# The first third of a hand-written order laid out anew, in a fused retention and wave-MLP kernel

## The chip, the cores and the metric

The kernel runs on one core of a Trainium2 chip. The metric is the device time of one execution in microseconds. The core's engines are TensorE (PE: matrix products and transposes), VectorE (DVE), ScalarE (ACT) and GpSimd (POOL); SyncE (SP) issues most of the transfers, ScalarE and GpSimd issue the others. All transfers share 16 DMA engines.

## The reference

Two stages. The first is a linear attention with a decay for each head, over q, k and v of shape 4 × 8 × 768 × 64. The second, on its output laid out as x of 4 × 768 × 512, is a mixing of phases over tokens and a mixing over channels.

```python
for t in range(S):
    state = gamma[None, :, None, None] * state + np.einsum('bhd,bhe->bhde', k[:, :, t], v[:, :, t])
    y[:, :, t] = scale * np.einsum('bhd,bhde->bhe', q[:, :, t], state)
...
theta = x @ w_theta
zr, zi = x * np.cos(theta), x * np.sin(theta)
y = np.einsum('ts,bsd->btd', w_tok_r, zr) + np.einsum('ts,bsd->btd', w_tok_i, zi)
u = x + y
return u + np.maximum(u @ w_ch, 0.0)
```

## The kernel before

The order of the work is not left to a scheduler. `ORDER` is a string of 929 tokens, and the last loop of the kernel calls the function that each token names, in that order. A token such as `ck.2.a` is a function (`ck`), a number (unit 2) and, where there is a choice, an engine: `a` ScalarE, `v` VectorE, `p` GpSimd, `s` SyncE. Each engine executes its own instructions in the order in which the tokens issue them; between engines, semaphores hold the data dependences. So the place of a token decides what stands behind it on its own engine, and nothing else.

**Attention.** The work is cut into 24 units: batch b, a third i of the tokens (256 of them) and half of the heads h, with n = 2 (3 b + i) + h. For each unit:

- `Lk`, `Lq`, `Lv` load 256 KB each of k, q and v. The loads of SyncE and ScalarE take turns on eight semaphores.
- `ck` casts k to bf16; `cq` casts q (in units 0 to 3, 7, 9 and 10, among others, `cqs` multiplies it with the decay instead); `cv` multiplies v with its decay. All three write what PE reads (`kqb`, `vb`).
- `Tk`, `Tq` transpose on PE into one PSUM tile, `E` copies it to SBUF (`kqT`).
- `A` makes the 16 small products of q and k (`at_ps`, one PSUM buffer), `m` masks them on VectorE (`at`, 1024 columns).
- `ST` adds up k-v states in columns of the PSUM banks R0 and R1 of the unit; `S0`, `S1` carry the state on to the next third of the tokens, and `SB.n.g` copies it to bf16 for `I`, the product of q with the old state. `Y` adds the product with `at` in the same banks.
- `XB` (after `cqs`) copies the result out of R0 or R1 to `xT`; `XA` (after `cq`) multiplies it with the decay on the way. The result of unit n stands in the banks beside the states of unit n + 1, so `I` of unit n + 1 can write to them only after `XB` or `XA` of unit n.

**Mixing.** For each tile C of 128 tokens: `Tx` transposes `xT` and `Ex` copies it (or `Dx` does both by DMA), `Hh` makes theta on PE with the weights `wth`, `CN` takes sine and cosine on ScalarE, `z` multiplies both with x. `Tw.r.t` transposes a row tile of a token weight matrix (r = 0 real, 1 imaginary), `Ew` copies it. `M.t.s` adds two products into row tile t; `u`, `Tu`, `Eu` (or `Du`), `O` and `f` are the channel mixing with the weights `wch`, and `SO` stores.

**Weights.** `Pth` loads w_theta, `Pch` w_ch, and `Pw.r.g` the token weights in groups of row tiles: g = 0 is row tile 0, g = 1 is row tiles 1 and 2, g = 2 is row tiles 3 to 5. GpSimd issues all of them, in order with its own operations, and they are cast from f32 to bf16 on the way.

**Others.** `const…` prepare constants; `const9` and `const8` are four activations each that fill the table `qx` (const8 256 columns, those of the first third of the tokens, const9 the 512 of the others), which `XA` alone reads; `const7` brings the table of the sine into ScalarE. `Z` is two products of zeros on PE, to nothing.

In the order before, the changed part has 338 tokens and ends at `M.4.5`; it holds the attention of units 0 to 8 in full and parts of units 9 and 10, and row tiles 0 to 2 of batch 0 with a part of tile 3.

Of the kernel before, what the change touches and what calls it, by code (L numbers as in the profile page):

```python
# [34 lines left out]
CN.3.0 Tx.4 CN.3.1 Ew.0.0.v S0.6.v XA.5.1 Ex.4.v Hh.4 CN.4.0 CN.4.1 Tw.0.1 M.0.1 Pw.1.1 z.3.v M.0.0
Tw.0.2 Pw.1.2 Ew.0.2.a SB.6.1.a Hh.5 z.4.p SB.6.0.p Lk.9.a M.0.3 ck.7.p cqs.7.p M.0.2 CN.5.1 CN.5.0
cq.8.v m.6 Ew.0.1.v Tw.1.1 Tw.1.2 Ew.1.1.v Lv.9.s M.0.4 M.1.0 Tx.5 Ew.1.2.v M.1.1 S1.6 Tk.7 M.1.4
Pch Ex.5.v z.5.v cv.7.v Tq.8 Tq.7 M.1.2 E.7.a M.0.5 I.6 Y.6 ST.7 A.7 ck.8.a u.0 S0.7.v m.7 XA.6.1
SB.7.1.a M.1.5 M.1.3 XA.6.0 Tw.1.3 M.2.5 Pw.0.2 M.2.3 u.1 S1.7 Tk.8 M.2.1 M.2.0 SB.7.0.v Ew.1.3.a
Tu.0 I.7 cv.8.v E.8.a Lk.10.s ck.10.p cv.9.p Y.7 ST.8 A.8 cqs.9.v ck.9.v M.2.4 Du.1 Eu.0.a XB.7.1.a  # L40
XB.7.0.v S0.8.v SB.8.0.v M.2.2 Tx.6 Tq.9 Tk.9 Lv.10.a cv.10.p Lq.10.s S1.8 u.2 m.8 O.0 E.9.a
SB.8.1.a Hh.6 Tw.1.4 I.8 Y.8 A.9 CN.6.0 Du.2 Lq.14.s CN.6.1 Ex.6.v f.0 ST.9 Tw.0.3 Hh.7 Ew.1.4.v
Ew.0.3.a S0.9.v Tw.0.4 M.3.0 Tw.1.5 CN.7.0 CN.7.1 M.3.2 Dx.7 M.3.1 M.3.5 M.3.3 Lv.12.s Lk.12.s
Ew.1.5.v XA.8.1 Ew.0.4.v Lq.12.s M.3.4 u.3 S1.9 Tw.0.5 Tk.10 M.4.5 cqs.10.p XA.8.0 m.9 M.4.3 Tq.10
SB.9.1.a SB.9.0.a I.9 O.2 Lq.11.s Lk.11.s E.10.a Lk.15.s Ew.0.5.v Lk.14.s Y.9 ST.10 A.10 z.7.p
Lv.11.s XB.9.1.a XB.9.0.a f.2 M.4.0 O.1 M.4.1 cqs.14.p m.10 S0.10.v f.1 cq.11.a ck.12.v M.4.4 M.4.2
Tu.3 Eu.3.a Dx.9 SB.10.0.a cqs.12.p u.4 Hh.9 Tq.11 ck.11.v Tu.4 z.6.v Eu.4.v ck.15.v M.5.0 M.5.4
Tk.11 E.11.a SB.10.1.p cv.11.p M.5.2 M.5.3 I.10 M.5.5 M.5.1 Lq.13.a A.11 Y.10 ck.14.v ST.11 CN.9.1
CN.9.0 SO.0.a Hh.8 u.5 S0.11.v z.9.v XB.10.0.v m.11 Dk.12 Tx.8 Tq.14 O.4 Lv.13.a SB.11.0.a Lq.15.s
Lk.13.s CN.8.1 Lk.18.a XB.10.1.a CN.8.0 SB.11.1.p cv.12.p Lq.16.s I.11 Tk.14 Ex.8.v A.12 Y.11 ST.12  # L50
f.4 Lv.15.s O.3 z.8.p E.14.a XA.11.0 XA.11.1 Hh.10 S0.12.a f.3 SB.12.0.v Tx.10 Tu.5 CN.10.1 Dx.11
Ex.10.v cq.13.p Lk.16.s Lv.17.s Hh.11 SO.2.s CN.10.0 m.12 S1.12 z.10.v Tk.15 M.6.1 M.6.2 M.6.0 M.6.3
CN.11.0 CN.11.1 M.7.3 SB.12.1.a Lk.17.a ck.13.a M.7.4 M.7.0 M.6.4 Dk.13 M.7.1 z.11.v M.6.5 SO.3.s
A.14 M.7.2 Eu.5.v I.12 Lv.14.s u.6 cqs.15.v M.7.5 M.9.3 Tq.15 ck.17.a E.15.a m.14 SO.4.a Lq.17.s
Lq.18.s Lk.21.s ck.16.a M.9.0 M.9.5 M.9.1 M.9.4 Lq.19.a M.9.2 Du.6 cv.13.v u.7 M.8.0 u.9 Y.12
cv.14.p ST.13 A.13 O.5 XB.12.1.a XB.12.0.a M.8.1 S0.13.a S1.13 M.8.4 M.8.3 SB.13.0.a SB.13.1.p
cq.16.p m.13 I.13 ck.18.a Y.13 ST.14 A.15 f.5 cq.17.v Lv.18.a M.8.5 M.8.2 XA.13.0 XA.13.1 S0.14.v
SB.14.0.p Lv.16.s Hh.13 S1.14 u.8 Tx.12 M.10.1 cv.15.p cv.17.p SB.14.1.p M.10.0 M.10.4 cqs.18.v
M.10.5 CN.13.0 CN.13.1 Hh.12 CN.12.1 I.14 m.15 Y.14 CN.12.0 ST.15 S0.15.v XB.14.1.a SB.15.0.a M.10.3
cv.16.v Dk.16 Dk.17 Du.7 Dx.13 M.10.2 Dk.18 O.6 SB.15.1.p XB.14.0.v S1.15 I.15 Y.15 ST.16 SO.5.a  # L60
cv.18.p f.6 S0.16.v A.16 M.11.4 SB.16.1.p M.11.1 Lq.21.a Ex.12.a z.12.p SB.16.0.a Lk.19.s Lk.20.s
XB.15.0.a u.10 z.13.p XB.15.1.a m.16 O.7 Du.10 I.16 Y.16 ST.17 f.7 A.17 Tu.8 Hh.15 CN.15.1 CN.15.0
Dx.14 M.11.2 Tx.15 Lv.22.s SO.7.s M.11.0 M.11.5 S0.17.v SB.17.0.p M.11.3 XA.16.1 m.17 XA.16.0
Ex.15.v Hh.14 SB.17.1.p z.15.p cq.19.p ck.21.p Eu.8.a ck.19.p I.17 u.11 Tu.11 A.18 Y.17 ST.18
# [7 lines left out]
cv.21.v u.14 A.21 ST.21 CN.19.0 CN.19.1 S0.21.v M.15.3 M.15.5 S1.21 m.21 XA.20.1 Hh.18 CN.18.1  # L72
CN.18.0 Dx.18 Dk.22 ck.23.a M.15.4 M.15.2 SB.21.0.p M.15.1 M.15.0 SB.21.1.v Lv.23.s Du.12 Dx.19
XA.20.0 O.9 f.9 I.21 Y.21 A.22 ST.22 M.16.1 cqs.23.p u.15 m.22 S0.22.v z.18.p z.19.p M.16.5
SB.22.0.p M.16.4 O.12 M.16.0 SO.8.a M.16.2 M.16.3 SB.22.1.p XB.21.0.a XB.21.1.a SO.11.s Du.14
cv.23.p Dk.23 f.12 Du.13 Dx.20 Dx.21 Hh.21 u.16 I.22 A.23 Y.22 ST.23 CN.21.0 CN.21.1 Hh.20 CN.20.1
# [6 lines left out]
Mh.1.0 Mh.1.4 u.22 O.18 Mh.1.3 SO.15.a f.19 M.20.0 M.20.1 Tuh.0 u.21 Du.22 Du.21 f.18 M.20.3 Euh.0
M.20.4 Mh.1.1 M.20.5 u.20 O.22 Mh.1.5 uh.1 f.22 Tu.20 SO.14.a SO.19.s Eu.20.a O.21 SO.18.a Tuh.1
Euh.1 f.21 Oa.0 Oa.1 fa.0 fa.1 Oh.0 Oh.1 SO.21.a SO.22.s SO.20.s fh.0 SOh.0 fh.1 SOh.1 Z.31
""".split()


# [558 lines left out]
```

## Time and profile before

| | |
|---|---|
| time, median of 3 runs | 165.81 us (165.0 to 166.0) |
| span of the profiled execution | 163.6 us |
| around the span, against the median | 2.2 us |
| PE busy | 155.2 us, 95% |
| VectorE, ScalarE, GpSimd busy | 114.0, 78.9, 74.3 us |
| bytes read, written | 25.69 MB, 6.29 MB |

The profiled execution has its own time, the span from its first to its last instruction; the runs are timed from outside, and the median lies 2.2 us above the span. Row 2 of the page cuts the span into 40 slices of 4.1 us, with a digit of tenths for each engine. In the timeline a line is a start, a length, the engine, the line of the kernel, the operation with its tiles, and in brackets the idle time before it with what ended it. `PE` is the products, `PEld` the loading of weights beside them.

### The profile page before, as it was taken

The page shows a single profiled execution, that of the slowest core. Times are in us where ns is not written, and L with a number is a line of the kernel's source. Part 1 is how long each engine was busy: PE and PEld are TensorE (multiplying, and loading weights), DVE is VectorE, ACT ScalarE, POOL GpSimd, SP SyncE. Part 2 cuts the span into 40 slices and gives each one's busy share as a digit, 9 for nine tenths or more (in the row PEclk, how much of TensorE's full clock was granted, in tenths as well). Part 3 has the DMA queues.
Part 4 walks back from the last instruction along what each step waited for, and adds up shares of the span by engine and source line. Part 5 has one row for each costly group of instructions (what it writes and reads, how often), then busy time and mean ns, then how long its engine had stood idle before and what let it go on. Part 6 is the DMA issues. An engine that isn't in the chain of part 4 may idle for free.

```text
span 163.6 us, 4928 instructions
## 1 busy us (share of the span) xinstructions
PE 155.2 (95%) x2034; PEld 87.2 (53%) x2034; DVE 114.0 (70%) x215; ACT 78.9 (48%) x140; POOL 74.3 (45%) x107
## 2 busy tenths in 40 slices
PE   5996889999999999999999999999999999999992
...
DMA  3999999999999999999999999999897548515546
GB/s 115 297 290 255 268 283 236 275 220 286 220 162 232 223 291 139 338 203 270 324 263 198 134 268 221 242 193 298 125 245 136 103 92 227 160 64 128 129 164 224
DMA packets 69062, 34.93 MB, mean 214 GB/s; under 512 B 26416, under 2 KB 66096, under 8 KB 69040
## 3 DMA queue, kind: packets, MB, share of 16 engines
...
q0 software_dynamic: 2688, 3.41, 12.1%
...
HBM read 25.69 MB, written 6.29 MB: 196 GB/s over the span
## 4 chain that ended last, share of the span: by engine, by line
PE 76%; DMA 8%; ACT 5%; POOL 3%; issue 2%; SPq 2%; DVE 1%; POOLq 0%; ACTq 0%
PE y_ps L509 36%; PE o_ps L536 11%; PE th_ps L469 10%; DMA kqf<-in_k_dram 8%; PE r_ps L423 3%; ACT qx L233 3%; PE w_ps L491 3%; PE at_ps L346 3%; PE r_ps L411 2%; PE kq_ps L316 2%; SPq L157 2%; PE y_ps L561 2%; ACT cs L476 1%; PE x_ps L455 1%; PE r_ps L373 1%
## 5 line engine op out<-in xcount | busy, mean ns | idle before, releaser
L509 PE MATMUL y_ps<-z,wtr 128*128 128x512 bf16 x138 | 52.4, 380 | 0.0
L509 PE MATMUL y_ps<-z,wti 128*128 128x512 bf16 x138 | 52.3, 379 | 0.0
L483 POOL TENSOR_TENSOR z<-cs,x_sb 128x1024 bf16<-128x1024 bf16 x12 | 25.5, 2136 | 17.9 <-ACT cs L476 10.0
L355 DVE TENSOR_TENSOR at<-at_ps,mask 128x1024 bf16<-128x1024 f32 x24 | 29.2, 1216 | 0.2
L469 PE MATMUL th_ps<-wth,xT 128*128 128x512 bf16 x96 | 24.5, 379 | 0.5 <-ACT cs L476 0.4
L516 DVE TENSOR_TENSOR u<-y_ps,x_sb 128x512 bf16<-128x512 f32 x23 | 15.8, 688 | 12.7 <-PE y_ps L509 12.6
L542 DVE SCALAR_TENSOR_TENSOR ot<-o_ps,u 128x512 f32<-128x512 f32 x22 | 15.1, 688 | 12.5 <-PE o_ps L536 12.4
L308 POOL TENSOR_TENSOR vb<-vf,vsc 128x512 bf16<-128x512 f32 x15 | 15.6, 1041 | 17.3 <-DMA vf<-in_v_dram 16.9
L476 ACT ACTIVATE cs<-th_ps,zerob 128x512 bf16<-128x512 f32 x24 | 16.4, 685 | 13.3 <-PE th_ps L469 8.8
L536 PE MATMUL o_ps<-wch,uT 128*128 128x512 bf16 x88 | 22.6, 379 | 0.0
L476 ACT ACTIVATE cs<-th_ps,halfpi 128x512 bf16<-128x512 f32 x24 | 16.3, 686 | 11.5 <-issue 5.4
L509 PEld LDWEIGHTS <-wtr 128*128 128x128 bf16 x138 | 13.5, 98 | 12.7
L509 PEld LDWEIGHTS <-wti 128*128 128x128 bf16 x138 | 13.5, 98 | 12.0 <-issue 0.2
L139 POOL CAST sbd<-s 64x256 bf16<-64x256 f32 (+1 forms) x21 | 10.1, 481 | 20.8 <-DVE s L391 17.7
L137 ACT COPY kqT<-kq_ps 128x1024 bf16<-128x1024 bf16 x12 | 12.1, 1012 | 11.9 <-PE kq_ps L316 11.9
L469 PEld LDWEIGHTS <-xT 128*128 128x128 bf16 x96 | 8.8, 98 | 8.7 <-issue 0.5
L137 ACT CAST kqb<-kqf 128x512 bf16<-128x512 f32 x16 | 9.6, 620 | 6.9 <-DMA kqf<-in_k_dram 6.3
L536 PEld LDWEIGHTS <-uT 128*128 128x128 bf16 x88 | 8.1, 98 | 8.3
L278 PE MATMUL zz<-zero 128*128 128x512 bf16 x30 | 10.3, 476 | 1.9 <-DVE zero L192 1.9
L423 PE MATMUL r_ps<-at,vb 64*64 64x128 bf16 x384 | 9.9, 221 | 1.6 <-DVE at L355 1.6
L316 PE MATMUL kq_ps<-ident,kqb 128*128 128x128 bf16 x120 | 11.2, 220 | 0.3 <-POOL kqb L302 0.3
L139 POOL CAST kqb<-kqf 128x512 bf16<-128x512 f32 x12 | 7.2, 612 | 8.5 <-DMA kqf<-in_k_dram 8.4
...
## 6 DMA issues: line engine op xcount, KB each, us to landing
...
```

The source lines that it names most:

```text
L137: nc.scalar.copy(dst, src)
L139: engines[e].tensor_copy(dst, src)
L308: engines[e].tensor_mul(in_blocks(vb), by_token(raw["vf", n]), _bcast_last(K["vsc"][:, i, :, h * HU:(h + 1) * HU], D))
L355: nc.vector.tensor_mul(at.rearrange("p g j a t -> p (g j) (a t)"), st["at_ps", n].rearrange("p g j a t -> p (g j) (a t)"), _bcast_mid(K["m ...
L423: nc.tensor.matmul(st["R", n + 1][c][g * D:(g + 1) * D, j * P:(j + 1) * P], st["vb", n][rows, lo:lo + D], st["at", n][rows, g, j, a, :], s ...
L469: nc.tensor.matmul(th_ps, st["xT", C][:, j, :], K["wth"][:, j, :], start=(j == 0), stop=(j == 3))
L476: nc.scalar.activation(st["cs", C][:, w, :], st["th_ps", C], AF.Sin, bias=K["zerob" if w else "halfpi"], scale=1.0)
L483: engines[e].tensor_mul(st["z", b][:, c], st["cs", C], _bcast_mid(x_of(C), 2))
L509: nc.tensor.matmul(st["y", t], K["wT"][r][:, s0, t0 * P:(t0 + 1) * P], st["z", b][:, s0, r, :], start=(done == 0 and r == 0), stop=(done = ...
L516: nc.vector.tensor_add(st["u", t], st["y", t], st["x", b][:, t0, :])
L536: nc.tensor.matmul(o_ps, st["uT", t][:, j, :], K["wch"][:, j, :], start=(j == 0), stop=(j == nD - 1))
L542: nc.vector.scalar_tensor_tensor(st["ot", t], st["o", t], 0.0, st["u", t], ALU.max, ALU.add)
```

## The change

Only `ORDER` changes, and of it only the first 338 tokens; from `M.4.3` on the 591 others are the same. The new part holds the same tokens, in another order, except that 42 of them name another engine. Each load keeps its issuer. The part was laid out over a replay that holds the load semaphores and lets VectorE and GpSimd exclude each other. In its first part:

```diff
-const4 Lq.1.a const9 Lk.1.s Z.39 const8 ck.0.p Tk.0 ck.1.a cqs.0.v cv.0.v Tq.0 E.0.v Lq.4.a ST.0
-Lk.4.a cqs.1.p Tq.1 Lq.2.s S0.0.v SB.0.1.v A.0 Lk.2.s SB.0.0.p cv.1.p Lv.2.s S1.0 Z.15 I.0 Z.27 m.0
-Tk.1 E.1.a cqs.2.v Z.34 cv.2.p Y.0 ST.1 XB.0.1.a S0.1.v S1.1 SB.1.0.a Pth Lq.3.s Z.18 XB.0.0.v Tq.2
-A.1 SB.1.1.a ck.2.a I.1 m.1 Y.1 ST.2 Tk.2 const7 Z.23 XB.1.0.v Lk.3.s E.2.v XB.1.1.v A.2 ck.3.p
-S0.2.v m.2 S1.2 SB.2.1.a Z.11 cqs.3.p Tq.3 Lv.3.s Tx.0 Tk.3 Z.3 ck.4.p Lv.4.s Lk.5.s Lq.5.s Lv.5.s
-Lq.6.s Lk.6.s Lv.6.s Lq.7.s E.3.a SB.2.0.v I.2 Y.2 XB.2.1.a Ex.0.a cv.3.v cq.4.p Tk.4 Lq.8.s A.3
-ST.3 Lk.7.s S0.3.v SB.3.0.a S1.3 Lv.7.s Lk.8.s Tx.1 Tq.4 SB.3.1.p cv.4.p m.3 Pw.1.0 XB.2.0.a Ex.1.a
-I.3 Lv.8.s E.4.a ck.5.a cq.5.a Y.3 Pw.0.0 ST.4 Hh.0 S0.4.v XB.3.0.v XB.3.1.v cv.5.v CN.0.1 A.4
-CN.0.0 Tq.5 Hh.1 Tk.5 SB.4.0.p SB.4.1.a Pw.0.1 Hh.2 m.4 E.5.v I.4 Y.4 ST.5 ck.6.a Tk.6 Tx.2 cq.6.a
...
+const4 Lq.1.a const9 Lk.1.s ck.0.p Lv.2.s cqs.0.v cv.1.p Lq.3.s Z.39 Lq.4.a Z.18 cqs.1.v Z.3 ck.1.a Tk.0
+cv.0.v Tq.0 E.0.a Tk.1 Z.15 ST.0 cv.2.p S0.0.v Lk.4.a Lq.2.s A.0 Tq.1 SB.0.1.p Z.34 SB.0.0.a cqs.3.p m.0
+S1.0 E.1.a I.0 const8 Y.0 Lk.2.s ST.1 Pth Lk.3.s cqs.2.v S0.1.v A.1 XB.0.0.a ck.3.p ck.2.p S1.1 Z.27
+Lk.5.s Tq.3 SB.1.1.a cq.4.p Lv.4.s Z.23 SB.1.0.a Tq.2 XB.0.1.a ck.4.p Tk.2 m.1 E.2.v const7 I.1 Y.1 ST.2
+S0.2.v Tk.3 S1.2 Lv.3.s XB.1.0.a A.2 Tk.4 SB.2.1.a m.2 SB.2.0.p XB.1.1.a I.2 E.3.a Tq.4 Lq.5.s E.4.v Y.2
+cv.3.p ck.5.p ST.3 Tx.0 S0.3.v XB.2.0.a XB.2.1.a cq.5.p S1.3 SB.3.0.a A.3 Tk.5 cv.4.p Tq.5 SB.3.1.a Z.11
+I.3 m.3 Lv.5.s Y.3 A.4 E.5.a Pw.1.0 ST.4 S0.4.v Pw.0.0 Tx.1 Ex.0.a Hh.0 Hh.1 Lk.6.s Lq.6.s XB.3.0.v
+SB.4.1.a Ex.1.a SB.4.0.p XB.3.1.v m.4 Tx.3 CN.0.0 I.4 Y.4 cv.5.p ST.5 ck.6.v CN.0.1 A.5 Hh.2 Ex.3.v
+z.0.v CN.1.1 Tx.2 Pw.0.1 CN.1.0 S0.5.v Pw.1.1 Tk.6 Lv.6.s cq.6.a XA.4.1 CN.2.0 XA.4.0 m.5 z.1.v Lq.7.s
+Lk.7.s SB.5.0.p SB.5.1.p Tq.6 cv.6.p Hh.3 E.6.a I.5 Y.5 Ex.2.v ST.6 A.6 CN.2.1 CN.3.0 CN.3.1 XA.5.0
+Pw.1.2 Tw.0.0 Ew.0.0.v S0.6.v Tw.1.0 Hh.4 Lv.7.s z.2.v Ew.1.0.a Tx.4 Ex.4.a Lk.8.s Tw.0.2 SB.6.0.p
...
```

The 42 tokens that change engine, by kind: the copies and products `E` 0, 4, 5, 7; `ck` 2, 5 to 10; `cq` 5, 8; `cqs` 1, 9; `cv` 3, 5, 8; `z` 0 and 4 (GpSimd to VectorE); `SB` of units 0, 2, 3, 5, 7, 8; `XB` of units 0 and 1; `Ex` 3, 4, 6; and seven `Ew`. `cv` 3, 5 and 8 go from VectorE to GpSimd, `E` 0 and 5 from VectorE to ScalarE, `E` 4 and 7 the other way.

More of the change, by code (lines that the diff above doesn't have):

```diff
@@ L35 @@
[L35 to L64, printed above, removed]
@@ new lines @@
+SB.4.1.a Ex.1.a SB.4.0.p XB.3.1.v m.4 Tx.3 CN.0.0 I.4 Y.4 cv.5.p ST.5 ck.6.v CN.0.1 A.5 Hh.2 Ex.3.v
+z.0.v CN.1.1 Tx.2 Pw.0.1 CN.1.0 S0.5.v Pw.1.1 Tk.6 Lv.6.s cq.6.a XA.4.1 CN.2.0 XA.4.0 m.5 z.1.v Lq.7.s
+Lk.7.s SB.5.0.p SB.5.1.p Tq.6 cv.6.p Hh.3 E.6.a I.5 Y.5 Ex.2.v ST.6 A.6 CN.2.1 CN.3.0 CN.3.1 XA.5.0
+Pw.1.2 Tw.0.0 Ew.0.0.v S0.6.v Tw.1.0 Hh.4 Lv.7.s z.2.v Ew.1.0.a Tx.4 Ex.4.a Lk.8.s Tw.0.2 SB.6.0.p
+CN.4.1 M.0.1 Lq.8.s Tw.0.1 z.3.v Lk.9.a XA.5.1 M.0.3 Ew.0.2.v Tx.5 CN.4.0 cqs.7.p Lv.8.s SB.6.1.a S1.6
@@ new lines @@
+Hh.5 Ex.5.v Tw.1.2 ck.8.p Ew.0.1.a Tw.1.1 M.0.2 m.6 Lq.9.s CN.5.1 CN.5.0 Lv.9.s Ew.1.1.v z.5.v I.6 M.0.0
+z.4.v Tq.7 M.1.2 Ew.1.2.a M.1.3 cv.7.v Lk.10.s M.1.0 M.1.1 M.0.5 Pw.0.2 Tw.1.3 ck.7.a Tk.7 M.0.4 M.1.5
+E.7.v Ew.1.3.a Y.6 Lv.10.a ST.7 A.7 u.0 S0.7.v cv.8.p XA.6.1 cq.8.a SB.7.1.a S1.7 Tk.8 SB.7.0.a M.1.4
+Tq.8 Tu.0 E.8.a XA.6.0 m.7 M.2.2 M.2.4 I.7 M.2.5 Y.7 A.8 ST.8 S0.8.v SB.8.0.a u.1 M.2.1 S1.8 Pch M.2.3
+XB.7.0.v M.2.0 u.2 ck.9.p Eu.0.a cqs.9.p Tw.1.4 SB.8.1.p Tq.9 Tk.9 XB.7.1.a Hh.6 Ew.1.4.a Du.1 Dx.7 Tx.6
```

60 lines of the change are left out of this document (40 added, 20 removed).

## The prediction

> **What bounds the kernel now.** I read the page first, then windows over the first third, then the chain, then the timeline engine by engine.
>
> ```profile
> span 163.6 us, 4928 instructions
> PE 155.2 (95%) x2034; PEld 87.2 (53%) x2034; DVE 114.0 (70%) x215; ACT 78.9 (48%) x140; POOL 74.3 (45%) x107
> PE   5996889999999999999999999999999999999992
> DMA  3999999999999999999999999999897548515546
> GB/s 115 297 290 255 268 283 236 275 220 286 220 162 232 223 291 139 338 203 270 324 263 198 134 268 221 242 193 298 125 245 136 103 92 227 160 64 128 129 164 224
> ```
>
> TensorE is 95% busy. Its only thin stretch is the first seven slices, exactly what the change lays out anew. The DMA row is full there as well, so two things can bind in this third. The windows put sizes on it:
>
> ```profile
> 8.00:12.00 4.00, 3.73 (x86) 2.25 (x82) 3.50 (x8) 2.91 (x6) 2.13 (x4) 1.00 1.22 290
> 12.00:16.00 4.00, 2.50 (x77) 1.60 (x75) 3.29 (x7) 2.59 (x5) 3.18 (x5) 1.00 1.22 264
> 16.00:20.00 4.00, 3.66 (x80) 2.56 (x79) 2.74 (x7) 2.58 (x5) 1.35 (x3) 1.00 1.15 256
> 20.00:24.00 4.00, 3.20 (x66) 1.99 (x65) 3.31 (x7) 3.97 (x8) 3.37 (x6) 1.00 1.21 291
> 24.00:28.00 4.00, 3.61 (x76) 2.44 (x75) 2.98 (x5) 3.12 (x7) 3.83 (x3) 1.00 1.15 239
> 28.00:32.00 4.00, 3.99 (x80) 2.65 (x79) 3.58 (x9) 3.93 (x7) 0.77 (x2) 1.00 1.15 277
> 32.00:54.80 22.80, 22.80 (x320) 14.37 (x318) 18.19 (x40) 13.84 (x23) 9.21 (x10) 1.00 1.22 217
> ```
>
> The first figure after the length is PE busy. From 8 to 28 us PE is idle 0.27 + 1.50 + 0.34 + 0.80 + 0.39 = 3.3 us; from 28 us to the end of the changed part (54.8) it never waits. The clock is 1.00 throughout. So 3.3 us, 2%, is what a better order can win here, unless it also turns warm-up matmuls into work. The chain says what the front waits for:
>
> ```profile
> 8.85 0.43 ACT kqb L137
> 9.32 6.61 DMA kqf<-in_k_dram
> 19.31 5.96 DMA kqf<-in_k_dram
> 25.37 1.14 ACT kqb L137 x2
> ```
>
> It runs through two loads: k of unit 4, landing at 15.93, and k of unit 6, landing at 25.27. In front of PE stands the stream of loads.
>
> **The change part by part.** No operation is added or removed: both orders have the same 338 entries ahead of an identical remainder, with 42 copies and products moved to another engine. All matmuls stay, fillers too. This gives a cut at which both orders can be compared. When the old order reaches the transposes Tw.0.1 and the new one Tw.0.2, each has the same PE work behind it and the same left: ten Tw, 25 M, three Hh and so on. The old one stands there at 32.16:
>
> ```profile
> 32.16 0.50 PE L491 MATMUL w_ps<-ident,row 128*128 128x128 bf16 x6
> ```
>
> Behind it PE has no gap, so when Tw.0.2 starts in the new order decides the sum.
>
> *Loads.* Issuers stay, but SP now issues v2 and q3 ahead of q2 and k2, and k5 ahead of v4 and v3.
>
> ```profile
> 6.22 0.69 DVE L302 TENSOR_TENSOR kqb<-kqf,qsc 128x512 bf16<-128x512 f32 x1 [3.26 <-DMA kqf<-in_q_dram]
> 12.62 0.93 POOL L173 DMA_DIRECT2D wth<-in_moe_w_theta_dram  x1
> row<-in_moe_w_tok_r_dram POOLq DMA_DIRECT2D x1, 384.0 KB, 8.5
> row<-in_moe_w_tok_i_dram POOLq DMA_DIRECT2D x1, 384.0 KB, 7.7
> SPq L157 <- DMA kqf<-in_q_dram: 4.5, 1, 4.5
> ```
>
> The third load (q0) lands by 6.2 and the fourteenth (k4) at 15.93: 0.88 us a load, and 256 KB at the page's 290 GB/s is 0.90. The weights are f32 in memory and bf16 on landing, so they read twice what the rows name: wth is four loads' worth, a 384 KB row tile three. The last row is the load semaphores: there are eight, so a load waits for the landing of the eighth before it, and SP stood 4.5 us at v4 until q4 had landed. The engines stayed full meanwhile. Landings follow the order of issue at that pace. With it the new order lands v2 9.7, q3 10.6, q2 and q4 11.5 to 12.4, k2 13.3, k3 14.2, k5 15.1, k4 16.0, v4 16.9, v3 17.8, v5 22.8 (the same eighteen loads and wth lie ahead of it in both orders). Nothing is gained in total; unit 2 completes at 13.3 instead of about 11.5, units 4 and 5 in part earlier.
>
> *Units 0 to 3.*
>
> ```profile
> 3.95 4.90 ACT L233 ACTIVATE qx<-pos,lscale,lgp 128x512 f32<-128x512 f32 x8 [0.43 <-POOL lgp L228]
> 8.85 0.62 ACT L137 CAST kqb<-kqf 128x512 bf16<-128x512 f32 x1
> 10.56 1.01 ACT L137 COPY kqT<-kq_ps 128x1024 bf16<-128x1024 bf16 x1 [1.09 <-PE kq_ps L316]
> 13.07 1.28 ACT L252 ACT_TABLE_LOAD   x1
> 7.99 0.69 DVE L139 COPY kqT<-kq_ps 128x1024 bf16<-128x1024 bf16 x1 [0.47 <-PE kq_ps L316]
> 9.38 1.22 DVE L355 TENSOR_TENSOR at<-at_ps,mask 128x1024 bf16<-128x1024 f32 x1
> 15.98 1.17 POOL L139 CAST kqb<-kqf 128x512 bf16<-128x512 f32 x2 [0.82 <-DMA kqf<-in_k_dram]
> 13.86 0.42 PE L423 MATMUL r_ps<-at,vb 64*64 64x128 bf16 x16 [1.11 <-DVE at L355]
> 15.56 0.42 PE L346 MATMUL at_ps<-kqT 64*64 64x128 bf16 x16 [0.39 <-DVE kqT L139]
> 18.10 0.42 PE L423 MATMUL r_ps<-at,vb 64*64 64x128 bf16 x16
> 20.01 1.22 DVE L355 TENSOR_TENSOR at<-at_ps,mask 128x1024 bf16<-128x1024 f32 x1
> ```
>
> E.0 goes from VectorE (0.69) to ScalarE (1.01) and there behind ck.1.a, which needs k1 and ends at 9.46 as before. So kqT of unit 0 is ready at 10.5 instead of 8.7, and m.0 starts at about 10.9 instead of 9.38: 1.5 us late. On PE, Tk.1 now stands ahead of ST.0 and waits for the same ck.1.a. Then const8 (four of the eight activations in the 4.90 us, half as wide: about 2.0) runs on ScalarE after E.1, ahead of XB.0.0, SB.1 and XB.0.1, which I.1 needs: I.1 not before 15.6. Likewise ck.2.p stands on GpSimd behind ck.3.p, which waits for k3 (14.2): 14.3 + 0.61 + 0.61 = 15.5 for Tk.2, with Y.1 and ST.2 queued behind on PE. So Y.1 starts near 15.9 where the row has 13.86, A.2 near 16.7 instead of 15.56. PE idles about 1.4 us ahead of Tk.2, as it did 1.11 ahead of Y.1. The activation-table load of const7 (1.28) then delays XB.1.0 and SB.2.1 to 18.0, so Y.2 comes at 18.8 instead of 18.10. m.3 comes at 20.2 against 20.01: the loss is nearly made up.
>
> *Units 4 to 6.* Here the new order gains. ck.5 and Tk.5 no longer stand behind Hh.0 and Hh.1: Tk.5 at 19.9 where it was at 24.16. The two 2.1 us z products leave GpSimd for VectorE at 0.69:
>
> ```profile
> 24.16 0.39 PE L316 MATMUL kq_ps<-ident,kqb 128*128 128x128 bf16 x4
> 24.17 2.12 POOL L483 TENSOR_TENSOR z<-cs,x_sb 128x1024 bf16<-128x1024 bf16 x1 [0.70 <-ACT cs L476]
> 29.06 0.68 DVE L483 TENSOR_TENSOR z<-cs,x_sb 128x1024 bf16<-128x1024 bf16 x1
> 33.82 1.22 DVE L355 TENSOR_TENSOR at<-at_ps,mask 128x1024 bf16<-128x1024 f32 x1
> ```
>
> They are covered by cv.3 and cv.5 (0.69 each) going the other way; with the durations of the same operations in the old order, VectorE reaches m.4 at 23.6, m.5 at 27.4 and m.6 at 34.0 against 33.82, so it neither gives nor takes. Walking PE on in the same way (each wait is for the m before it or for SB and XB of the unit before), Hh.0 starts at 22.6, after wth's landing at about 21.5, A.6 ends near 29.6, Hh.4 at 31.15, Tx.4 at 31.4: PE would be at the cut 0.8 us early.
>
> *The row tiles.* Tw.0.2 needs Pw.0.1, issued by GpSimd.
>
> ```profile
> 20.30 1.04 POOL L308 TENSOR_TENSOR vb<-vf,vsc 128x512 bf16<-128x512 f32 x1
> 22.76 0.71 POOL L182 DMA_DIRECT2D row<-in_moe_w_tok_r_dram  x1
> 27.24 1.53 POOL L182 DMA_DIRECT2D row<-in_moe_w_tok_i_dram  x2
> ```
>
> Now it lands at 22.76 + 8.5 = 31.3, just ahead of 32.16. In the new order Pw.0.1 stands behind cv.5.p, which needs v5 (22.84) and SB.4.0: 23.25 + 1.04 = 24.3, or 1.5 us later; and SP, no longer held up at v4, has q7, k7 and v7 out by then, where only q7 was ahead before. 3 us of its own bytes aside, the delay of 8.5 us was backlog; with two more loads ahead I place the landing at 31.3 + 2 × 0.88 = 33.1. Bounds: alone on the engines it takes 0.79 MB / 290 GB/s = 2.7 us and lands at 27.0, and PE goes on at 31.4 (0.8 gained); with k8 and q8 also ahead it is 34.9 (2.7 lost). I take 33.1, since both 384 KB rows (8.5 and 7.7) lie by a full backlog and far from 2.7. The second tile, Pw.1.1, issued right behind instead of at 27.24, lands by 35.7, and Tw.1.2 comes up at 35.8: no further wait.
>
> [...]
>
> *Later.* Pw.0.2 goes ahead of Pch, and O.0, which needs wch, to the end of the part: I put both at nothing, covered by the M in between; were wch late, it would cost up to its own 4 × 0.88 = 3.5. PE behind the part is full, so a shift passes through.
>
> *Sum.* 33.2 - 32.16 = +1.0 us: span 164.6. The profiled execution has a span of 163.6, the median is 165.81: 2.2 us lie around it. So 166.9.
>
> **The rivals.**
>
> *The front closes up (faster).* One mechanism: the row tiles land in the engines' gaps, in time for PE, which then takes the early Tk.5 and Tq.5 as cover for the waits of 20 to 28 us. It decides from the point at which Pw.0.1 lands before 31.4. Price: at least 0.8; if all 3.3 us go, 162.5; the middle, 2.0, gives 163.8. For it: PE does come early to the cut. Against: the same bytes at full DMA.
>
> *q5 behind wth (slower).* In the new order q5 (issued when q4 lands, 12.4) and wth (issued behind cqs.3.p, 12.3) are a tie. If wth goes first, q5 lands 4 × 0.88 = 3.5 us later, near 22.2; cq.5.p stands on GpSimd ahead of cv.4.p and of all four row tiles, so cv.4, ST.4 and the tiles come some 2.5 us later: 166.9 + 2.2 = 169.1. Nothing in the rows breaks the tie.
>
> *Nothing moves.* Row tiles and PE shift together, since the bytes ahead of Tw.0.2 are the same: 165.8. The full DMA row speaks for it, the later issue against it.
>
> **How the numbers follow.** Forecast 0.38 (own range 165.3 to 168.5), faster rival 0.25, slower rival 0.27, nothing 0.10. About 1% is what a measurement of this kernel tells from no change. Over 1% faster (below 164.1): 0.20, from the first rival. Over 1% slower (above 167.5): 0.10 of the forecast and 0.25 of the rival, 0.35. Within: 0.45. The range reaches from most of the first rival, 163.4, to the second, 169.2.
>
> **What would show it.** Right: m.0 starting near 10.9, Y.1 near 15.9 behind Tk.2, Tk.5 near 20, a PE wait of 1 to 2 us at L491 near 32 put down to a row tile, and no gap from there to 55. Wrong: L491's group t0 = 1, 2 starting before 31.5 (row tiles in time), or ST.4 later than 23 (q5 behind wth), or PE gaps beyond 36.

## Result and the profile after

The changed kernel is slower: 172.78 us, median of four runs (171.35 to 173.38), against 165.61 us; the ratio is 1.043, 95% interval [1.038, 1.048]. The profiled execution took 171.35 us with a span of 169.6 us, 6.0 us more than the 163.6 of before. Here and below a median is over all runs, while a ratio leaves out those more than 1.5% above the fastest run of their kernel. Line numbers are 2 lower than in the kernel before.

From the page, the busy time of each engine, and the rows of slices of PE and of its granted clock:

```profile
PE 156.3 (92%) x2034; PEld 87.7 (52%) x2034; DVE 114.0 (67%) x202; ACT 80.9 (48%) x146; POOL 76.8 (45%) x114
PE   5968769957999999999999999999999999999992
PEclk9999978999999999999999999999999999999999
```

Thin slices now reach to the tenth, where they ended with the sixth before, and in the sixth and seventh the clock is lower. The windows over this part (PE busy is the first figure after the length, the granted clock the third from the end):

```profile
16.00:20.00 4.00, 3.44 (x112) 2.46 (x108) 3.19 (x6) 2.89 (x7) 2.43 (x4) 1.00 1.23 245
20.00:24.00 4.00, 1.91 (x46) 1.30 (x41) 1.42 (x2) 2.23 (x5) 2.02 (x3) 0.95 1.19 302
24.00:28.00 4.00, 4.00 (x59) 2.37 (x52) 2.42 (x5) 2.44 (x6) 3.32 (x6) 0.63 1.13 239
28.00:32.00 4.00, 4.00 (x94) 2.76 (x94) 3.73 (x7) 3.95 (x7) 2.12 (x5) 1.00 1.14 281
32.00:36.00 4.00, 2.49 (x68) 1.77 (x58) 3.75 (x7) 3.56 (x7) 2.39 (x4) 1.00 1.14 213
36.00:40.00 4.00, 2.15 (x21) 1.39 (x22) 3.86 (x4) 1.68 (x4) 3.03 (x4) 1.00 1.15 227
40.00:60.80 20.80, 20.80 (x300) 12.89 (x298) 15.27 (x29) 12.68 (x22) 7.18 (x7) 1.00 0.81 157
```

From 20 us on three windows are thin: 20 to 24, 32 to 36 and 36 to 40 us. From 40 us to the end of the changed part PE never waits. A fourth window looks full and is not: in 24 to 28 us PE is busy 4.00 of 4.00 us, but at a clock of 0.63, so that the same products take longer. Cut at the change of the clock, the window of half speed is exactly this long:

```profile
20.17:23.58 3.41, 1.32 (x19) 0.85 (x14) 1.42 (x2) 1.64 (x5) 1.60 (x3) 1.00 1.17 305
23.58:26.99 3.41, 3.41 (x60) 2.20 (x58) 2.04 (x5) 2.04 (x4) 2.73 (x6) 0.50 1.15 266
26.99:30.40 3.41, 3.41 (x73) 2.27 (x72) 2.52 (x8) 3.17 (x6) 1.64 (x3) 1.00 1.09 241
```

What PE waited for between 20 and 40 us (in total, times, longest):

```profile
PE kq_ps L314 <- POOL kqb L137: 2.1, 1, 2.1
PE y_ps L507 <- DVE z L481: 1.5, 1, 1.5
PE w_ps L489 <- DMA row<-in_moe_w_tok_r_dram: 1.4, 1, 1.4
```

These are Tq.5 waiting for GpSimd's cast of q5, M.0.3 waiting for VectorE's product z.3, and Tw.0.2 waiting for the row tile Pw.0.1. The chain of waits leads to the first of them:

```profile
12.21 9.71 DMA kqf<-in_q_dram
21.93 0.05 issue
21.98 0.63 POOL kqb L137
22.60 0.05 issue
22.65 0.40 PE kq_ps L314 x4
...
25.45 2.55 PE th_ps L467 x8
```

Load q5 was issued at 12.21 us and landed at 21.93. In the kernel before it landed no earlier, at 21.96 us, but its cast stood on ScalarE, where ck.5 and cq.5 are one row:

```profile
21.65 1.14 ACT L137 CAST kqb<-kqf 128x512 bf16<-128x512 f32 x2
```

In the changed kernel the cast stands on GpSimd, ahead of cv.4 and of all row tiles, as GpSimd's timeline shows:

```profile
21.98 0.62 POOL L137 CAST kqb<-kqf 128x512 bf16<-128x512 f32 x1 [2.61 <-DMA kqf<-in_q_dram]
22.55 1.04 POOL L306 TENSOR_TENSOR vb<-vf,vsc 128x512 bf16<-128x512 f32 x1
...
26.73 0.79 POOL L180 DMA_DIRECT2D row<-in_moe_w_tok_r_dram  x1
```

The last row issues Pw.0.1. The view of transfers has it with its size and its time to landing:

```profile
row<-in_moe_w_tok_r_dram POOLq DMA_DIRECT2D x1, 384.0 KB, 9.4
```

So it is issued at 26.73 and lands at 36.13 us, where it was 22.76 and 31.3. The last wait is on VectorE; in the timeline its z.2 and z.3 stand in one row, and below it GpSimd's rows of the same time:

```profile
34.08 4.79 DVE L481 TENSOR_TENSOR z<-cs,x_sb 128x1024 bf16<-128x1024 bf16 x2
34.88 1.03 POOL L300 TENSOR_TENSOR kqb<-kqf,qsc 128x512 bf16<-128x512 f32 x1
35.88 0.60 POOL L137 CAST kqb<-kqf 128x512 bf16<-128x512 f32 x1
36.43 0.80 POOL L180 DMA_DIRECT2D row<-in_moe_w_tok_r_dram  x1
37.26 1.05 POOL L306 TENSOR_TENSOR vb<-vf,vsc 128x512 bf16<-128x512 f32 x1
```

z.2 takes 0.68 us, z.3 then 4.19: from 34.68 to 38.87, which is 0.56 us after GpSimd's cv.8 ended (37.26 + 1.05).

The account at M.4.5, where the orders meet again (54.41 us before, 60.43 after, +6.02): PE's idle times up to there, the first 1.92 us at the start included, sum to 10.1 us against 5.2, which is 4.9; the other 1.1 us are in the products. The half clock is the large term there: the same products from Tq.5 to Tx.3 take 5.19 us here (22.65 to 27.84) and 3.62 at full clock in the experiment e3_fill below, 1.6 us more; so elsewhere some 0.4 us went the other way, which was not followed. Behind M.4.5 the shift stays: the last operation of VectorE begins 6.05 us later than before.

### The profile page after: what moved, and what is told of

Same layout as the page of the kernel before. It is cut to its first block, busy times and chain, and to the rows that moved or that the text cites. A ratio compares the mean times of both kernels' runs of the same rounds, so it can differ in the third digit from the quotient of the medians.

```text
span 169.6 us, 4941 instructions
## 1 busy us (share of the span) xinstructions
PE 156.3 (92%) x2034; PEld 87.7 (52%) x2034; DVE 114.0 (67%) x202; ACT 80.9 (48%) x146; POOL 76.8 (45%) x114
## 3 DMA queue, kind: packets, MB, share of 16 engines
q0 software_dynamic: 2688, 3.41, 11.6%
## 4 chain that ended last, share of the span: by engine, by line
PE 74%; DMA 10%; DVE 6%; issue 4%; SPq 3%; POOL 2%; ACT 1%; POOLq 0%; ACTq 0%
PE y_ps L507 34%; PE o_ps L534 11%; PE th_ps L467 10%; DMA kqf<-in_q_dram 6%; DMA vf<-in_v_dram 4%; PE r_ps L421 4%; SPq L155 3%; PE at_ps L344 3%; PE kq_ps L314 2%; DVE z L481 2%; PE r_ps L409 2%; PE w_ps L489 2%; PE y_ps L559 2%; POOL kqb L137 1%; PE x_ps L453 1%
## 5 line engine op out<-in xcount | busy, mean ns | idle before, releaser
L306 POOL TENSOR_TENSOR vb<-vf,vsc 128x512 bf16<-128x512 f32 x18 | 18.9, 1057 | 16.1 <-DMA vf<-in_v_dram 15.6
L481 POOL TENSOR_TENSOR z<-cs,x_sb 128x1024 bf16<-128x1024 bf16 x10 | 21.1, 2127 | 10.1 <-ACT cs L474 9.3
L467 PE MATMUL th_ps<-wth,xT 128*128 128x512 bf16 x96 | 25.2, 390 | 0.1
L137 POOL CAST sbd<-s 64x256 bf16<-64x256 f32 (+1 forms) x24 | 11.6, 482 | 28.6 <-DVE s L389 22.5
L474 ACT ACTIVATE cs<-th_ps,halfpi 128x512 bf16<-128x512 f32 x24 | 16.4, 688 | 11.6 <-issue 5.1
L481 DVE TENSOR_TENSOR z<-cs,x_sb 128x1024 bf16<-128x1024 bf16 x14 | 13.5, 977 | 0.7 <-DMA x_sb<-xT 0.6
L137 POOL CAST kqb<-kqf 128x512 bf16<-128x512 f32 x15 | 8.9, 608 | 9.9 <-PE w_ps L489 6.3
L314 PEld LDWEIGHTS <-kqb 128*128 128x128 bf16 x120 | 8.0, 98 | 7.1 <-POOL kqb L137 3.0
```

The source lines that it names most:

```text
L137: engines[e].tensor_copy(dst, src)
L306: engines[e].tensor_mul(in_blocks(vb), by_token(raw["vf", n]), _bcast_last(K["vsc"][:, i, :, h * HU:(h + 1) * HU], D))
L314: nc.tensor.transpose(st["kq_ps", n][:, 4 * w + x, :], st["kqb", n][:, w, x * P:(x + 1) * P], K["ident"])
L467: nc.tensor.matmul(th_ps, st["xT", C][:, j, :], K["wth"][:, j, :], start=(j == 0), stop=(j == 3))
L474: nc.scalar.activation(st["cs", C][:, w, :], st["th_ps", C], AF.Sin, bias=K["zerob" if w else "halfpi"], scale=1.0)
L481: engines[e].tensor_mul(st["z", b][:, c], st["cs", C], _bcast_mid(x_of(C), 2))
```

## The experiments

The theory: q5 lands later than forecast, together with the weights wth; what costs is that its cast stands on GpSimd ahead of cv.4 and the row tiles, that the pause of PE halves the clock, and that GpSimd's operations keep z.3 out. The rival: the new order of the loads is the cause by itself. All times in one view (span and M.4.5 from the profiled execution):

| kernel | median us | ratio to before, 95% | span us | M.4.5 us |
|---|---|---|---|---|
| before | 165.4 to 165.6 | 1 | 163.6 | 54.41 |
| after | 172.78 | 1.043 [1.038, 1.048] | 169.6 | 60.43 |
| e1_q5_aside | 167.08 | 1.010 [1.006, 1.014] | 165.2 | 56.09 |
| e2_pool_clear | 168.39 | 1.019 [1.014, 1.024] | 166.6 | 57.40 |
| e3_fill | 168.08 | 1.015 [1.012, 1.018] | 166.9 | 57.47 |
| e4_pth_late | 173.49 | none | 171.9 | 62.74 |
| e5_both | 173.69 | 1.040 [1.036, 1.044] | 169.8 | 60.58 |
| e6_fill_clear | 168.31 | 1.018 [1.014, 1.021] | 166.0 | 56.87 |
| e7_both_row | 169.03 | 1.022 [1.017, 1.027] | 167.6 | 58.42 |
| e8_old_q5_pool | 168.98 | 1.021 [1.019, 1.023] | 167.1 | 57.91 |
| e9_old_collide | 166.26 | 1.005 [1.003, 1.006] | 165.1 | 55.88 |
| e10_both_cv8p | 166.41 | 1.006 [1.004, 1.008] | 164.9 | 55.70 |
| e11_old_q5_fill | 167.95 | 1.016 [1.013, 1.019] | 167.2 | 58.02 |

The runs of e4_pth_late went apart by clock, too far for an interval: 169.29 us at a mean clock of 0.999, 173.36 to 174.90 at 0.968 to 0.980.

**e1_q5_aside**: the cast of q5 leaves GpSimd; its transpose moves a little back.

```diff
-XB.2.1.a cq.5.p S1.3 ... cv.4.p Tq.5 SB.3.1.a ... A.4 E.5.a ... Tx.1 Ex.0.a
+XB.2.1.a S1.3 ... cv.4.p SB.3.1.a ... A.4 Ex.0.a cq.5.a ... Tx.1 Tq.5 E.5.a
```

> The changed order with cq.5 moved from GpSimd to ScalarE and Tq.5, E.5 moved behind Tx.1 on PE and ScalarE, so that nothing stands behind q5. Theory A (q5 comes in step with wth, and what stands behind cq.5.p is late: cv.4, ST.4 and all row tiles): the PE wait of 2.09 us at Tq.5 goes, Pw.1.0 is issued near 20.5 instead of 23.54, Pw.0.1 near 24.5 instead of 26.73, Tw.0.2 starts near 34 instead of 36.17, and the span falls by 1.8 to 2.7 us from 169.6. Theory B (the row tiles are late because the transfers ahead of them are the same bytes whenever they are issued): Pw.0.1 lands at 36 again, PE waits at Tw.0.2 instead, and the span falls by under 0.5.

q5 landed no earlier (21.81 us), yet the time fell by 5.7 us. cv.4 began at 19.42 us instead of 22.55, Pw.0.1 was issued at 24.94 and landed at 32.71, and Tw.0.2 stood at 32.77. Between 20 and 40 us PE's longest waits were 0.5 us, and no window had a clock below 1.00 in the profile (one of the other three runs had a mean of 0.99). Where q5's cast stands carries most of the loss; the gain is larger than either size I had given, since the clock went back up with it and z.3 took 1.78 us, not 4.19.

**e2_pool_clear**: GpSimd's three operations beside z.3 go to VectorE and ScalarE.

```diff
-cqs.7.p ... ck.8.p ... m.6 ... cv.7.v ... ck.7.a ... cv.8.p
+m.6 cqs.7.v ... cv.7.v cv.8.v ... ck.7.a ck.8.a
```

> The changed order with cqs.7 and cv.8 moved from GpSimd to VectorE (behind m.6 and cv.7) and ck.8 to ScalarE (behind ck.7), so that GpSimd has no product or copy beside z.3. Theory A (z.3, which took 4.19 us where the others took 0.68, is shut out by GpSimd's operations): z.3 takes 0.7 to 1.3 us, M.0.3 no longer waits 1.48 us, Tw.0.2 stays at 36.2 and the span falls by 1.4 to 1.9 us. Theory B (z.3 waits for something else, a landing or a semaphore): it takes about 4 us again and the span stays within 0.5 us of 169.6.

```profile
32.63 1.38 DVE L481 TENSOR_TENSOR z<-cs,x_sb 128x1024 bf16<-128x1024 bf16 x2
```

In this row of VectorE's timeline z.2 and z.3 together take 1.38 us, as two products of 0.69 do: that GpSimd's operations keep z.3 out is shown. The time is not as clean: PE's pause at Tq.5 was 1.81 us here and the clock stayed at 1.00 in the profile, so 3.0 us of span hold part of the clock too.

**e3_fill**: five empty products in the pause.

```diff
-Tk.5 cv.4.p Tq.5
+Tk.5 Z.40 Z.41 Z.42 Z.43 Z.44 cv.4.p Tq.5
```

> The changed order with ten more products of zeros (five Z, 2.15 us) on PE ahead of Tq.5, in the 2.09 us in which it stood still; no work of the result is changed. The granted clock of 24 to 28 us, 0.63, should return to 1.00 in every theory. Theory A (the row tile Pw.0.1 sets Tw.0.2, and of the low clock only what delays ST.4 counts): the two Hh take 1.7 us instead of 2.75, but PE waits longer at Tw.0.2, and the span falls by 0.3 to 0.6 us. Theory B (the low clock is itself a main part of the loss): the span falls by 1.2 to 1.8 us.

Nothing but PE's pause is filled: q5, GpSimd and the tiles stay late (Pw.0.1 lands at 35.16 us, 36.13 in the changed kernel), and yet the median falls by 4.7 us. Its windows:

```profile
20.00:24.00 4.00, 4.00 (x76) 2.39 (x69) 1.42 (x2) 2.34 (x6) 2.40 (x4) 1.00 1.17 301
24.00:28.00 4.00, 4.00 (x99) 2.54 (x88) 3.67 (x9) 3.77 (x8) 3.18 (x5) 1.00 1.07 250
```

The clock was 1.00 in all four runs, where all four of the changed kernel had 0.98 or 0.99. One such window of 3.41 us at half clock is 1.7 us, 1% of the span; so a mean of 0.98 means about two of them (an estimate from these rows). z.3 also met less: 2.34 us.

**e4_pth_late**: wth is issued behind ck.4, at 16.42 us instead of 12.29.

```diff
-ST.1 Pth Lk.3.s ... ck.4.p Tk.2
+ST.1 Lk.3.s ... ck.4.p Pth Tk.2
```

> The changed order with the load of wth moved on GpSimd from behind cqs.3.p to behind ck.4.p (issued near 16.5 instead of 12.3). Theory A (q5 was late because its packets took turns with those of wth): q5 lands near 18.6 instead of 21.93, PE does not wait at Tq.5, wth lands between 22.5 and 24 and Hh.0 waits up to 1 us for it; the row tiles are issued 2 to 3 us earlier; the span falls by 1.0 to 2.5 us. Theory B (q5 was late by its own place behind v4 and v3 and the semaphores): q5 lands at 21 to 22 again and the span does not fall.

q5 landed at 19.95 instead of 21.93 us and Tq.5 waited for nothing: wth had delayed q5 by 2.0 us. But wth itself then landed at 25.60 and the wait moved, and GpSimd's operations met z.3 as before (4.18 us); so the time did not fall, against theory A. What PE waited for, longest first:

```profile
PE y_ps L507 <- DVE z L481: 3.0, 1, 3.0
PE th_ps L467 <- DMA wth<-in_moe_w_theta_dram: 2.1, 1, 2.1
```

The windows show the same half clock behind the pause, and once more behind the wait for z.3; the second and third row are cut at the changes of the clock:

```profile
24.00:28.00 4.00, 2.36 (x8) 0.94 (x8) 1.65 (x3) 1.87 (x4) 2.52 (x4) 0.82 1.15 266
26.59:30.00 3.41, 3.41 (x57) 2.16 (x59) 1.02 (x2) 2.91 (x5) 0.00 (x0) 0.50 1.14 255
40.24:43.65 3.41, 3.21 (x19) 2.02 (x18) 1.99 (x4) 0.79 (x2) 0.00 (x0) 0.50 1.16 225
```

**e5_both**: e1_q5_aside and e2_pool_clear together (both diffs above).

> The edits of e1_q5_aside and e2_pool_clear together: cq.5 on ScalarE, Tq.5 later, and GpSimd's three products cqs.7, ck.8, cv.8 on VectorE and ScalarE. Theory A (the loss is GpSimd and PE standing behind q5, plus the lower clock after that pause, plus z.3 kept out by GpSimd): nothing is left but the later row tile. e1_q5_aside had Tw.0.2 at 32.77 us and z.3 at 1.78 us with 0.48 us of wait before M.0.3; here z.3 takes 0.69 us, M.0.3 does not wait, M.4.5 begins at 55.0 to 55.6 us (e1_q5_aside 56.09, before 54.41), span 164.2 to 164.9 us against 163.6 before. Theory B (the parts overlap, so that the second one mended gives nothing): as e1_q5_aside, span 165.2 us.

Both theories missed. Up to M.1.1 (39.09 us, e1_q5_aside 39.62) the kernel was ahead as theory A has it, and M.0.3 waited for nothing. What VectorE and PE waited for from 38 us on:

```profile
DVE vb L306 <- POOL kqb L137: 4.9, 1, 4.9
PE at_ps L344 <- DVE kqT L137: 3.6, 1, 3.6
```

The first row names GpSimd as releaser, though GpSimd had long been done: what came was v8, at 44.14 us. I had put cv.8 on VectorE ahead of the copy E.7, and v8 lands later here than in e2_pool_clear (40.68). There it had been issued at 25.89 us, here at 27.75; what else delays it was not followed. One product that waits for a load stopped VectorE, and PE 3.57 us behind it; from 44 to 48 us the mean clock was 0.62. It is the mistake of the change once more, on another engine.

**e6_fill_clear**: e3_fill and e2_pool_clear together.

> The edits of e3_fill and e2_pool_clear together: PE is kept busy with empty products while it waits for q5, and GpSimd's three products near z.3 are on other engines; q5 still holds GpSimd until 21.9 us. What is left is the lateness of the row tiles and of the work behind Tq.5. Theory A (clock and exclusion are taken away, the 2 us behind q5 stay): no half clock, z.3 0.69 us, Pw.0.1 lands near 35.1 us as in e3_fill and Tw.0.2 begins then, 2.3 to 3.0 us later than the cut of before; M.4.5 at 56.7 to 57.4 us, span 165.9 to 166.6 us. Theory B (the exclusion and the clock are the whole loss): span 163.6 to 164.5 us.

Theory A's numbers: M.4.5 at 56.87 us, span 166.0, z.3 0.78 us, clock 1.00 (only Tw.0.2 came earlier than it said, at 34.25 us). With clock and exclusion mended, the lateness of GpSimd and of the row tiles still costs 2.5 us at M.4.5. Against e3_fill alone the profiled span is 0.9 us shorter (166.0 and 166.9), but the median did not move (168.31 and 168.08): what the exclusion still costs there, four runs of each do not resolve.

**e7_both_row**: e5_both, and Pw.0.1 directly behind Pw.0.0.

```diff
-Pw.0.0 Tx.1 ... Tx.2 Pw.0.1 CN.1.0
+Pw.0.0 Pw.0.1 Tx.1 ... Tx.2 CN.1.0
```

> As e5_both, and the row tile Pw.0.1 is issued right behind Pw.0.0 instead of behind cv.5.p. It is issued at 21.6 us instead of 24.9 and lands at 29.5 to 31.5 us instead of 32.7, so that Tw.0.2 waits for nothing. Theory A (the row tile is the last term that is left): Tw.0.2 begins at 32.5 us or before, M.4.5 0 to 0.5 us earlier than in e5_both, span 163.7 to 164.5 us. Theory B (the 0.8 us of issue on GpSimd ahead of SB.4.0 and cv.5 delays I.4 and ST.5 by as much, and PE waits there instead): span as e5_both or up to 0.8 us longer.

The tile landed at 30.15 us and Tw.0.2 began at 32.77, in e5_both at 32.88: with q5 aside, the tile binds no more. M.1.1 began at 38.99 us, in e5_both at 39.09, so up to there the 0.8 us of theory B do not show. The time behind it again holds the wait for v8 (2.78 us of PE at A.7), so it says nothing on theory A's gain.

**e8_old_q5_pool**: the kernel before, with one move.

```diff
-SB.3.1.p cv.4.p ... ck.5.a cq.5.a Y.3
+SB.3.1.p cq.5.p cv.4.p ... ck.5.a Y.3
```

> The kernel before with one move: the cast cq.5 goes from ScalarE (behind ck.5) to GpSimd, ahead of cv.4. q5 lands at 21.96 us in the kernel before, as it does in the changed one (21.93 us). Theory A (what costs is where q5's cast stands, not when q5 lands): cq.5 on GpSimd runs 22.0 to 22.6 us, cv.4 ends at 23.6 instead of 21.34 us, PE pauses some 1.9 to 2.1 us ahead of ST.4, all row tiles are issued 2.3 us later; if the pause also brings the half clock, 1.3 to 1.6 us more. Span 165.5 to 167.5 us against 163.6. Theory B (the new order of the loads is the cause): span 163.4 to 164.0 us.

The timeline of GpSimd and then of PE:

```profile
22.15 0.61 POOL L139 CAST kqb<-kqf 128x512 bf16<-128x512 f32 x1 [1.98 <-DMA kqf<-in_q_dram]
22.73 1.04 POOL L308 TENSOR_TENSOR vb<-vf,vsc 128x512 bf16<-128x512 f32 x1
...
23.82 0.43 PE L373 MATMUL r_ps<-vb,kqb 64*64 64x64 bf16 x16 [2.15 <-POOL vb L308]
```

And the window behind it:

```profile
24.00:28.00 4.00, 3.78 (x46) 1.91 (x43) 2.78 (x5) 1.84 (x4) 2.45 (x5) 0.62 0.99 214
```

This is the run that tells theory and rival apart. In the old order of the loads q5 landed at the same time as ever (22.00 us), and the one cast on GpSimd made the same pause (2.15 us), the same clock (0.62), and 3.5 us at M.4.5. All four runs had a clock of 0.99. The rival, which gave no change here, falls as the cause of the whole; what the new order of the loads costs by itself, no run shows.

**e9_old_collide**: the kernel before, with GpSimd's cqs.7 and ck.7 ahead of z.4.

```diff
-Pw.1.2 Ew.0.2.a ... z.4.p SB.6.0.p Lk.9.a M.0.3 ck.7.p cqs.7.p
+Pw.1.2 cqs.7.p ck.7.p Ew.0.2.a ... z.4.p SB.6.0.p Lk.9.a M.0.3
```

> The kernel before, with GpSimd's cqs.7 and ck.7 moved ahead of z.4 (behind the row tile Pw.1.2), so that they run while VectorE makes z.2 and z.3: cqs.7 when q7 has landed (30.6 us), ck.7 when k7 has landed (32.7 us). In the kernel before z.2 takes 0.69 us (30.95 to 31.64) and z.3 0.68 us (32.88 to 33.56), with GpSimd idle from 28.8 to 33.6 us. Theory A (a GpSimd product keeps VectorE's product of two SBUF tiles out until it ends, in whatever kernel): z.2 ends 0.55 to 0.7 us after cqs.7's end, so takes 1.0 to 1.7 us; z.3 beside the cast ck.7 takes up to 1.3 us. M.0.3, at 34.55 us, has room for that, so the time changes by -0.2 to +0.6 us. Theory B (the 4.19 us of z.3 come from something else, such as its operands arriving late): both stay at 0.69 us.

The timeline of VectorE, then of GpSimd:

```profile
30.60 0.42 DVE L441 TENSOR_TENSOR xT<-r_ps,qx 128x256 bf16<-128x256 f32 x1 [0.20 <-PE r_ps L373]
30.96 0.80 DVE L483 TENSOR_TENSOR z<-cs,x_sb 128x1024 bf16<-128x1024 bf16 x1
...
30.17 1.03 POOL L302 TENSOR_TENSOR kqb<-kqf,qsc 128x512 bf16<-128x512 f32 x1 [1.21 <-DMA kqf<-in_q_dram]
32.41 0.61 POOL L139 CAST kqb<-kqf 128x512 bf16<-128x512 f32 x1 [1.21 <-DMA kqf<-in_k_dram]
```

A small effect only, because the loads came earlier than I had reckoned: cqs.7 ran until 31.20 and z.2 ended 0.56 us later, at 31.76 (0.80 us instead of 0.69); ck.7 missed z.3 altogether. The XA product in the first row, with one operand in PSUM, took its usual 0.42 us in the midst of cqs.7. That is in line with the exclusion, and too small to carry it. The time rose by 0.8 us all the same, past theory A's 0.6: PE waited 1.16 us up to 50.60 us for a product of v on GpSimd, behind a load of k that landed at 48.81. Why the moved products delay that load was not followed.

**e10_both_cv8p**: as e5_both, but cv.8 stays on GpSimd.

> As e5_both, but cv.8 stays on GpSimd. In e5_both cv.8 stood on VectorE ahead of the copy E.7 and waited 4.91 us for v8, which landed at 44.14 us; until then e5_both was ahead of e1_q5_aside by 0.53 us (M.1.1 at 39.09 against 39.62 us). Theory A (q5's place, the clock and the exclusion are the loss, and e5_both lost by the new wait alone): M.4.5 at 55.4 to 55.7 us, span 164.4 to 164.8 us, no half clock. Theory B (taking the three products off GpSimd costs by itself further on): span 165.2 us or more.

The timeline of VectorE (z.2 and z.3) and of GpSimd (cv.8):

```profile
32.14 1.38 DVE L481 TENSOR_TENSOR z<-cs,x_sb 128x1024 bf16<-128x1024 bf16 x2
43.35 1.03 POOL L306 TENSOR_TENSOR vb<-vf,vsc 128x512 bf16<-128x512 f32 x1 [9.65 <-DMA vf<-in_v_dram]
```

And PE's longest waits from 8 to 60 us:

```profile
PE r_ps L409 <- POOL kqb L300: 1.1, 1, 1.1
PE kq_ps L314 <- ACT kqb L135: 1.1, 2, 0.9
PE r_ps L409 <- ACT sbd L135: 0.8, 2, 0.5
```

GpSimd now waits 9.65 us for v8 and nobody minds. M.4.5 stands at 55.70 us (0.39 before e1_q5_aside), the clock is 1.00, the span 164.9: theory A, 0.1 us past its range for the span. With q5's cast aside, the pause gone and z.3 free, 6.4 of the 7.2 us are back. What is left is 0.9 us against the runs of before beside it (165.47), 1.3 us at M.4.5. PE's idle times up to M.4.5, without the first 1.92 us, sum to 4.9 us here and to 3.3 us in the kernel before, and the largest are those of the last three rows, before 22 us; whether the rest lies there, and so in the new order of units 0 to 3, was not tried. This is the best of the variants of the change, and it does not beat the kernel before.

**e11_old_q5_fill**: e8_old_q5_pool with five empty products ahead of ST.4.

```diff
-Y.3 Pw.0.0 ST.4
+Y.3 Z.40 Z.41 Z.42 Z.43 Z.44 Pw.0.0 ST.4
```

> As e8_old_q5_pool (the kernel before with q5's cast on GpSimd ahead of cv.4), with five empty products on PE ahead of ST.4, as long as its pause of 2.15 us. GpSimd, the loads and the row tiles are as late as there; only the pause of PE is filled. e8_old_q5_pool: Hh.0 1.89 us, clock 0.62 in 24 to 28 us, M.4.5 3.50 us later than before, span 167.1 us. Theory A (of the 3.5 us, the pause itself costs 2.15 less the 0.39 us of a later wait that it swallows, and the half clock behind it 1.3 to 1.7): clock 1.00, Hh.0 1.03 us, M.4.5 1.7 to 2.2 us later than before, span 165.3 to 165.9 us. Theory B (the half clock is a companion and costs nothing, the lateness of GpSimd costs all 3.5 us): span 167 us.

The window behind the filled pause:

```profile
24.00:28.00 4.00, 3.95 (x62) 2.18 (x56) 3.42 (x6) 2.85 (x6) 3.41 (x5) 1.00 1.02 235
```

And PE's timeline further on:

```profile
32.53 0.45 PE L491 MATMUL w_ps<-ident,row 128*128 128x128 bf16 x5
34.62 0.23 PE L491 MATMUL w_ps<-ident,row 128*128 128x128 bf16 x1 [1.63 <-issue]
```

Full clock, Hh.0 at 1.04 us, and I.4 2.27 us later than before. The profiled execution, 168.90 us, then lost 1.63 us between the fifth and the sixth transpose of one row tile, where no wait stands in the program; so its span of 167.2 us decides nothing. The spans of the other three runs were 165.9 to 166.4 us: up to 0.5 us past theory A's range, and under theory B's 167. Against e8_old_q5_pool the median is 1.0 us lower, 1.2 us without the execution that stalled: that is what half the clock costs there.

## Where the prediction was right and where wrong

**Units 0 to 3: right.** m.0 came at 10.84 us (10.9 said), Y.1 at 15.81 (15.9), A.2 at 16.62 (16.7), Tk.5 at 20.16 (19.9); only m.3, at 20.86, was 0.7 us later than said, and the wait ahead of Tk.2 was 0.59 us, not 1.4. The loads up to then too: v2 9.58 (9.7), k2 13.19 (13.3), v4 16.82 (16.9), v3 17.69 (17.8).

**Loads: the step that failed.** The forecast let q5 follow v3 at 0.88 us a load, ahead of wth, near 18.7 us. It landed at 21.93, and wth 0.4 us behind it, at 22.30. The two had been called a tie, and most of wth went first:

```profile
q0 software_dynamic: 406, 0.42, 107.6%
q1 hardware_dynamic: 137, 0.06, 15.0%
```

These are the packets by queue between 17.7 and 20.0 us: q0 holds GpSimd's transfers, here wth, q1 holds SP's. wth has three packets of four. e4_pth_late moved wth away, and q5 came 2.0 us earlier, of the 3.2 us that the forecast was off. In that run no packet of wth moved before q5 had landed (q0 is empty from 16.4 to 20.0 us), so the other 1.2 us are not wth's; where they come from stays open. What makes the lateness dear is the place of the cast, as e1_q5_aside and e8_old_q5_pool show: the forecast's sum had nothing waiting behind cq.5.p. The rival "q5 behind wth" had this step, with q5 near 22.2 us and the tiles 2.5 us later, which is 26.8 for Pw.0.1; it was issued at 26.73. Its chance was 0.27, against 0.38 for the forecast; the rows of before gave nothing to turn that round.

**The two queues.** Between 33 and 36 us the trace counts nearly as many packets of GpSimd as of SP, 328 and 318; between 17.7 and 20.0 us it counts 406 and 137, though SP had five loads under way (q5, v5, k6, q6 and v6, issued from 12.21 to 17.29 us). The forecast placed Pw.0.1 by the backlog of the 8.5 us row, and for the row tiles that held: it took 9.4 us from issue to landing where 8.8 was said.

**Row tiles: right in mechanism.** The wait at L489 for a row tile, 1.4 us, was named, as was the order of GpSimd's queue; only its start was 2.4 us off, by the step above. Tw.0.2 stood at 36.17 us, the rival's 35.4 plus 0.8.

**Units 4 to 6: that VectorE "neither gives nor takes" was wrong.** The two products of z that came to VectorE were priced at 0.69 us, and they do take that. What the sentence left out is what stands on GpSimd in their place: three operations in a row, with an issue between, shut z.3 out for 3.5 us. M.0.3 and Tx.5 paid 1.48 + 0.21 = 1.7 us. z.3, with both inputs in SBUF, ended 0.55 or 0.56 us behind GpSimd's last operation in the changed kernel, in e1_q5_aside and in e3_fill, and took 0.69 us in e2_pool_clear, without the three operations; XA, with PSUM on one side, took its usual 0.42 us beside one in e9_old_collide. The prediction has no term for this.

**The clock: not in the sum at all.** The clock was 1.00 all through the first third before, and was taken for granted. It cost 1.6 us in the products from Tq.5 to Tx.3 of the profiled execution, and more in two of the other runs, whose mean clock was 0.98. The stretch of half clock lasted 3.41 us (23.58 to 26.99 us), as each of the two in e4_pth_late did; those begin 13.65 us apart, four times as much (26.59 and 40.24 us). PE did not stand still all through the 3.41 us ahead of the drop: it was busy 1.32 of them.

**The sum.** +1.0 us was forecast, and +6.0 came. The rival's 169.1 us lacks 3.7 us against the median, and 2.25 us against the profiled 171.35: 0.8 at the cut and 1.7 behind it, less 0.4 since here 1.8 us and not 2.2 lie around the span; 0.2 us stay unexplained. The 1.7 us are z.3's, against the prediction's "no gap from there to 55". "Later: nothing" held to 0.03 us. Two of the three signs named for "wrong" came up: ST.4 stood at 24.48, and PE waited beyond 36 us.
